# Two attention layers and two Fourier layers on one core: larger q/k pieces from step 234, and two more projection pieces before the end of the attention

## The chip, the cores and the metric

One core of a Trainium2 chip runs the whole program. The metric is the device time of one execution in microseconds (us), the median of several. Engines are named as in the profile: PE (matrix products), PEld (its weight loads), DVE (vector), ACT (activation), POOL, and SP, which here only issues DMA transfers.

## The reference

`x` has 2048 rows of 640 numbers. Four sublayers run one after the other, with `_A_ref` (attention) and `_B_ref` (Fourier mixing) used twice each:

```python
def _A_ref(x, wqkv, wo):                      # H = 32 heads of Dh = 20
    qkv = (x @ wqkv).reshape(B, S, 3, H, Dh).transpose(2, 0, 3, 1, 4)
    q, k, v = qkv[0], qkv[1], qkv[2]
    p = softmax(einsum("bhqd,bhkd->bhqk", q, k) * Dh ** -0.5)
    o = einsum("bhqk,bhkd->bhqd", p, v)
    return o.transpose(0, 2, 1, 3).reshape(B, S, D) @ wo

def _B_ref(x, dft_seq_re, dft_seq_im, dft_hid_re, dft_hid_im):
    a = einsum("bsd,ed->bse", x, dft_hid_re);  b = einsum("bsd,ed->bse", x, dft_hid_im)
    return einsum("ts,bse->bte", dft_seq_re, a) - einsum("ts,bse->bte", dft_seq_im, b)

x = A_x
x = x + _A_ref(_layernorm(x), A_wqkv, A_wo)
x = x + _B_ref(_layernorm(x), B_dft_seq_re, B_dft_seq_im, B_dft_hid_re, B_dft_hid_im)
x = x + _A_ref(_layernorm(x), A_wqkv, A_wo)
x = x + _B_ref(_layernorm(x), B_dft_seq_re, B_dft_seq_im, B_dft_hid_re, B_dft_hid_im)
```

## The kernel before, in words

The program has two equal layers, each an attention and a Fourier part. A layer runs in stages.

**Prologue.** The rows of x are normalised and transposed (`xt`), and q and k of the first 128 columns and half of v are computed.

**Attention** (`Attention.sweep`). There are 512 steps: 8 groups of 4 heads, 4 blocks of 512 query columns (`qb`), 16 blocks of 128 key rows (`kc`). A step has two *scores* (`s` in the tables: two matmuls into one of three PSUM tiles `psc`, and after them one exponential on ACT, `e<-psc`, into one of seven buffers `e`) and one *values* (`v`: four matmuls, which the chip runs as eight, that add `e` times `v` to `acc`). After `kc` 15, DVE empties `acc`, divides by the row sums and POOL stores the result `o` to DRAM. PE's order is the order in which these calls are written down, one after the other.

**Filling work** stands between the steps on PE. The remaining columns of q and k (`pqk<-xt,wqk`) are made in units of 15 matmuls of 512 columns, each unit ending in a small matmul for row norms (`pn<-sq,ind`). `pieces(…, n)` cuts a unit into pieces of n. Up to step 234 (`THIN` is 236) a written-out string sets the order: `f` is a piece, `n` a norm. This part is called *dense* below. From there on before.py puts one piece of 5 at steps `(n - 1) % 16` in 2, 7, 12 (`due`), 33 pieces, and leaves the rest to the rule in `sweep`.

**Projection pieces.** From step 448 the table `tail` gives strings for 5 to 8 steps each, with one `f` in each. Such a piece is `Project.begin(n, i)`: 9 matmuls of 320 columns (`py<-wo,o`) that multiply three fifths of the attention's output for row tile n, half i, by `wo`; DVE adds the result to the residual rows `xr`. There are ten pieces (row tiles 0 to 4, two halves each).

**Projection stage** (`Project.run`). For row tiles 0 to 15, two halves each, PE does what is left of the product: 6 matmuls a half for tiles that were begun, 15 for the others. DVE adds it to `xr` (`L1007`), then the pair of row tiles is stored to DRAM (`d_x<-xr`, in `moments`) and normalised and folded for the Fourier part. SP issues in program order, pair by pair: a load of `xr` three pairs ahead, which reuses the buffer of the pair before and so waits for that pair's store; after pairs 1 and 3 eight loads of `o` (`fetch`) for the row tiles 8 to 11 and 12 to 15; then the pair's own store.

**Fourier part.** PE multiplies by the two DFT matrices. Its products start when the folded rows are there.

Things that run beside all this: DVE's comparisons of the DFT matrices (`compare`), and `tasks`, one at every second step, which load and split `wo` and other weights after the last q/k piece.

Of the kernel before, what the change touches and what calls it, by code (L numbers as in the profile page):

```python
# [19 lines left out]
ND = D // 128  # L20
NT = S // 128
# [18 lines left out]
def mha_fnet_kernel(ctx, tc, x_in, wqk, wv, wo, seq, hid, nat_seq, nat_hid, out):  # L40
# [33 lines left out]
    def bank(tag, shape, name):  # L74
        return pools["pool"].tile(list(shape), F32, name=name, tag=tag)
# [60 lines left out]
    class Qkv:  # L136
# [119 lines left out]
        def begin(s, first, kq, vals, room, given):  # L256


            s.first, s.room, s.given, s.w = first, room, given, {}
            for k in range(2):  # L260
                if given:
                    s.raw[k * ND] = given.wraw[k]
                else:
                    s.load(k)
            s.wvraw = [vals(f"v{NT - 1 - dc}", [HD], F32, "wvraw") for dc in range(ND)]
            if given:
                s.load_values()
# [117 lines left out]
        def work(s):  # L385

            order = [ND + 1, 1, ND + 2, 2, ND + 3, 3, ND + 4, 4]
            w = {0: s.w1}

            def chunk(i):  # L390
                c = order[i]
                for tb in range(NB):
                    p = bank("fill", [128, 512], "pqk")
                    for more in pieces([s.product(p, w[i], tb, dc) for dc in range(ND)], 8 if (i, tb) < (5, 1) else 5):
                        if more:
                            yield True
                    sq = s.keep(p, c, tb, True, s.fill)

                    def after():
                        s.norms(bank("fill", [H, 512], "pn"), c, tb, sq)  # L400
                        s.made.add((c, tb))
                        if tb == NB - 1:
                            s.made.add(c)
                            if i + 1 < len(order):
                                w[i + 1] = s.weights(s.fill("w", [2, ND, 128], F32R, "wqk"), order[i + 1], True)
                            if i + 2 < len(order):
# [12 lines left out]
            s.made.add("v")  # L419
            for i in range(4, 8):  # L420
                yield from chunk(i)

            s.silent = True
            r = s.bounds()
            ok = const.tile([128, 1], F32, name="ok", bufs=2)
            V.tensor_scalar(ok[:H], r[:H, 2:3], (GUARD / SCALE) ** 2, None, op0=OP.is_le)

            def after():
                p = bank("fill", [1, 1], "pok")
                PE.matmul(p, ok[:H], one[:H], start=True, stop=True)  # L430
                V.tensor_scalar(s.flag, p, float(H), None, op0=OP.is_equal)
            yield after
# [25 lines left out]
    class Attention:  # L458
# [98 lines left out]
        def sweep(s, shift, begin, fill=lambda n: None, plan=None, block=None, compare=lambda n: None):  # L557
            done = calm = n = 0

            def opened(n):  # L560
                g, qb, kc = s.steps[n]
                begin(n, g, qb, kc)
                last = qb == NB - 1
                if kc == (7 if last else 10 if g in LATE else 4) and not (last and g == H // 4 - 1):
                    s.qload(*((g, qb + 1) if not last else (g + 1, 0)), shift)
                if last and g + 1 < H // 4:
                    for f, j in {1: [(0, 0)], 9: [(0, 1)], 11: [(1, 0)]}.get(kc, []):
                        s.kload(g + 1, f, j)
                if qb == 0 and kc == 0 and g:
                    s.kload(g, 1, 1)  # L570

            while n < len(s.steps):
                opened(n)
                order = plan and plan(n)
                if order:

                    while done < n - 1:
                        s.values(done)
                        done += 1
                    t = 2 * n  # L580
                    for c in order:
                        if c == "s":
                            m, j = divmod(t, 2)
                            if not j and m > n:
                                opened(m)
                            s.scores(m, j)
                            if j:
                                compare(m)
                            t += 1
                        elif c == "v":  # L590
                            s.values(done)
                            done += 1
                        else:
                            (block if c == "f" else fill)(t // 2)
                    n = t // 2
                    continue
                s.scores(n, 0)
                s.scores(n, 1)
                more, owed = fill(n) and n >= 2 and n + 1 < len(s.steps), n - 1 - done
                compare(n)  # L600
                n += 1
                if plan and n <= s.THIN:
                    count = owed + 1
                elif more and owed < 3:
                    calm = n + 1
                    continue
                else:
                    count = min(owed, 1)
                    if owed > 1 and (done + 1) % NT and n > calm:
                        calm = n + 1  # L610
                        count = 2
                for _ in range(count):
                    s.values(done)
                    done += 1
            for n in range(done, len(s.steps)):
                s.values(n)

        def run(s, done, project, check):
# [2 lines left out]
            s.work, s.blocks, s.after, s.rest, s.more, s.landed = True, 0, None, 0, False, 0  # L621


            tail, n = {}, 448
            for steps in (6, 7, 6, 8, 6, 6, 6, 6, 5, 8):
                tail[n] = {5: "sssfssvssvvsssvv", 6: "sssfssvssvssvvsssvv", 7: "sssfssvssvssvssvvsssvv",
                           8: "sssfssvssvsvssvssvssvssvv"}[steps]
                n += steps

            def due(n):  # L630
                return s.blocks < 58 or s.blocks >= 91 or (n - 1) % NT in (2, 7, 12)

            def block(n):
                if not s.work:
# [22 lines left out]
            def plan(n):  # L657
                if n in tail:
                    return tail[n]
                if s.blocks >= 58 or s.after:  # L660
                    return
                whole = 32 <= s.blocks < 48
                if n % 4 == 1 and n + (4 if whole else 8) < s.THIN and (whole or s.blocks % 2 == 0):
                    return "sssfsssvvssvv" if whole else "ssfsssvvsssvvsssfssvvsssnvv"
# [22 lines left out]
            def begin(n, g, qb, kc):  # L687
# [17 lines left out]
                for f in project.early.get(n, []):  # L705
                    f()

            s.sweep("b", begin, fill, plan, block, compare)
            assert not s.work and not later and not tasks and not project.parts, (len(later), len(tasks))

# [233 lines left out]
    class Project:  # L944
        def __init__(s, att, src, dst):
            s.att, s.src, s.dst, s.w, s.raw = att, src, dst, {}, {}
            s.sum = {}
            s.oh, s.x, s.xn, s.rs, s.f, s.g, s.nb, s.na = {}, {}, {}, {}, {}, {}, {}, {}

            s.begun, s.parts = set(), [lambda n=n, i=i: s.begin(n, i) for n in range(5) for i in range(2)]  # L950
            s.early = {474: [lambda: s.fetch(0, 0, 1)], 486: [lambda: s.fetch(1, 0, 0)], 503: [lambda: s.fetch(0, 1, 1)]}

        def weights(s, dc):

# [662 lines left out]
```

## Time and profile before

| what | value |
|---|---|
| median of 3 runs | 2460.21 us (2456.98 to 2460.39) |
| the profiled execution's own time | 2460.17 us |
| its span, first to last instruction | 2458.3 us |
| PE busy | 2428.5 us (99% of the span) |
| ACT busy | 2117.6 us (86%) |
| DVE busy | 995.3 us (40%) |
| exponentials `e<-psc` | 2048, one per half step |
| mean granted TensorE clock | 0.998 |

A row of a timeline or of a group names line, engine, operation, the tile written and the tiles read, and the shape; `x8` is the number of instructions merged in the row. Times are from the span's start. PE's busy time is modelled from pipelined matmuls that overlap, so it says little; the time from the start of one row to the start of the next says what PE needed. Line numbers are those of before.py.

### The profile page before, as it was taken

The numbers are of one execution on the slowest core, as the hardware profiler recorded it, in microseconds if no ns is written. First come the engines' busy times: TensorE is split into PE (matmuls) and PEld (weight loads), VectorE is DVE, ScalarE is ACT, GpSimd is POOL, SyncE is SP. The second block draws the span as 40 slices with busy tenths as digits, with TensorE's granted clock in tenths as the row PEclk, the third lists the DMA queues.
The fourth block names the chain that finished last, engine by engine and source line by source line (L and its number), as shares of the span: only waits on it lengthen the run. The fifth ranks groups of instructions, "written<-read, shape, count | busy, mean of one in ns | idle before, by whom it ended". The sixth has DMA issues, their size and how long they took to land. (4 is left out here: it accounts for less than half of the span.)

```text
span 2458.3 us, 43836 instructions
## 1 busy us (share of the span) xinstructions
PE 2428.5 (99%) x16350; PEld 1174.1 (48%) x16350; DVE 995.3 (40%) x2198; ACT 2117.6 (86%) x2428; POOL 527.7 (21%) x1032
## 2 busy tenths in 40 slices
PE   8999999999999999999999999999999999999997
PEld 7644444443333333349885444454433333333596
DVE  6244442234343333427763444323333232323275
ACT  6699998899999999995457989888999999999762
POOL 2012211112111212115321212211112212222143
PEclk9999999999999999999999999999999999999999
DMA  5324231223232225318552332312222322252274
GB/s 184 101 89 126 81 113 51 77 69 109 74 96 89 88 86 168 96 44 284 193 182 96 112 102 85 117 53 69 79 82 57 93 64 68 57 151 83 67 255 185
DMA packets 128228, 262.64 MB, mean 107 GB/s; under 512 B 29937, under 2 KB 54289, under 8 KB 128005
## 3 DMA queue, kind: packets, MB, share of 16 engines
q1 hardware_dynamic: 89412, 159.89, 20.4%
q0 software_dynamic: 38592, 99.85, 12.8%
q8 instruction: 132, 2.16, 0.4%
q14 instruction: 92, 0.75, 0.1%
HBM read 175.29 MB, written 84.31 MB: 106 GB/s over the span
## 5 line engine op out<-in xcount | busy, mean ns | idle before, releaser
L525 ACT ACTIVATE e<-psc 128x1024 f32<-128x1024 f32 x2048 | 1919.4, 1059 | 109.9 <-PE psc L522 98.9
L533 PE MATMUL acc<-e,v 128*32 128x512 f32 x8192 | 1034.2, 600 | 0.4 <-DVE of L540 0.4
L522 PE MATMUL psc<-stq,stk 62*128 62x512 f32 x4096 | 745.3, 445 | 2.3 <-ACT e L525 1.1
L522 PEld LDWEIGHTS psc<-stq,stk 62*128 62x128 f32 x4096 | 333.9, 184 | 704.2 <-ACT e L525 563.8
L533 PEld LDWEIGHTS acc<-e,v 128*32 128x32 f32 x8192 | 217.5, 108 | 396.3 <-issue 357.5
L103 PE MATMUL pqk<-xt,wqk 128*128 128x512 f32 x1200 | 319.4, 407 | 0.5 <-ACT xt L90 0.2
L554 POOL DMA_DIRECT2D o<-oh x256 | 131.2, 521 | 828.7 <-DVE oh L549 816.8
L88 DVE CAST hl<-pqk 128x512 fp32r<-128x512 f32 x64 | 44.3, 692 | 597.8 <-PE pqk L103 597.8
L103 PEld LDWEIGHTS pqk<-xt,wqk 128*128 128x128 f32 x1200 | 213.1, 188 | 84.1 <-issue 39.6
L103 PE MATMUL pv<-wv,xt 128*128 128x320 f32 x960 | 151.3, 313 | 0.0
L103 PEld LDWEIGHTS pv<-wv,xt 128*128 128x128 f32 x960 | 141.1, 188 | 15.5 <-issue 9.7
L554 POOL DMA_DIRECT2D o<-ot x256 | 128.2, 509 | 1.8 <-issue 0.9
L540 DVE STREAM_TRANSPOSE of<-acc 128x512 f32<-128x512 f32 x64 | 45.8, 715 | 199.2 <-PE acc L533 199.2
L211 POOL DMA_DIRECT2D scrq<-hl x40 | 28.3, 706 | 429.6 <-DVE hl L91 240.1
L211 POOL DMA_DIRECT2D scrk<-hl x40 | 27.7, 693 | 390.1 <-DVE hl L91 280.6
L96 PE MATMUL py<-wo,o 128*128 128x320 f32 x320 | 101.3, 316 | 2.3 <-DVE xr L1007 1.3
L217 DVE TENSOR_REDUCE top<-pn 32x1 f32<-32x512 f32 x80 | 53.6, 677 | 121.0 <-PE pn L216 120.6
L803 DVE TENSOR_REDUCE far<-cq 128x1 f32<-128x512 f32 (+5 forms) x169 | 98.5, 584 | 5.7
L98 PE MATMUL py<-wo,o 128*128 128x320 f32 x320 | 99.1, 310 | 1.0 <-DMA o<-o 1.0
L97 PE MATMUL py<-wo,o 128*128 128x320 f32 x320 | 98.7, 308 | 0.0
L807 DVE TENSOR_TENSOR cq<-cq 128x512 f32<-128x512 f32 (+4 forms) x166 | 96.3, 580 | 4.2 <-DMA cq<-in_nat_seq_dram 3.5
L247 DVE COPY v<-pv 128x320 f32<-128x320 f32 x32 | 15.7, 489 | 161.3 <-PE pv L103 161.3
(201 smaller groups left out, 1750.7 us busy)
## 6 DMA issues: line engine op xcount, KB each, us to landing
cq<-in_nat_seq_dram POOLq DMA_DIRECT2D x64, 512.0 KB, 5.4
scrq<-hl POOLq DMA_DIRECT2D x40, 512.0 KB, 3.2
scrk<-hl POOLq DMA_DIRECT2D x40, 512.0 KB, 3.2
stq<-scrq SPq DMA_DIRECT2D x256, 80.0 KB
stk<-scrk SPq DMA_DIRECT2D x128, 160.0 KB
o<-o SPq DMA_DIRECT2D x32, 384.0 KB
stq<-scrq SPq DMA_DIRECT2D x256, 40.0 KB
stk<-scrk SPq DMA_DIRECT2D x128, 80.0 KB
```

The lines of the kernel that those rows point to most:

```text
L96: PE.matmul(out_ap, ah, bh, start=start, stop=False)
L97: PE.matmul(out_ap, ah, bl, start=False, stop=False)
L98: PE.matmul(out_ap, al, bh, start=False, stop=stop)
L103: yield lambda i=i, j=j, k=k: PE.matmul(out_ap, a[i], b[j], start=dc == 0 and k == 0, stop=dc == ND - 1 and k == 2)
L211: G.dma_start(s.scr["qk"[k]][c * 128:(c + 1) * 128, :, tb * 512:(tb + 1) * 512], hl.bitcast(F32))
L217: V.tensor_reduce(s.top[:H, c // ND, c % ND, tb:tb + 1], p, op=OP.max, axis=AX.X)
L522: PE.matmul(p[:, i], s.k[g, kc // 8, j][r, kc % 8 * 128:(kc % 8 + 1) * 128], s.q[g, qb, j][r], start=True, stop=True)
L525: A.activation(e, p, AF.Exp, scale=SCALE)
L533: PE.matmul(s.acc[32 * j:32 * j + 32], s.a.v[kc][:, v0:v0 + 32], s.e[n, j // 2][:, j % 2], start=kc == 0, stop=kc == NT - 1, skip_group_ch ...
L554: G.dma_start(s.o[k, h * DH:(h + 1) * DH, qb * 512:(qb + 1) * 512], hl[k][32 * j:32 * j + DH])
L803: V.tensor_reduce(to, x, op=OP.max, axis=AX.X, apply_absolute_value=True)
L807: V.tensor_tensor(y, x, y, op=op)
```

## The change

Three edits.

1. The last 11 q/k units: `pieces` now cuts every unit into 8 and 7, so there are 22 pieces after the 58th where there were 33. `plan` gives a written-out string for every eight steps from step 234 to 410, with one piece in each, in place of `due` and the rule in `sweep`. (For strings that begin otherwise than `ss`, `sweep` no longer catches up on values first.)
2. `tail` starts at step 432 and has twelve strings, and the twelve projection pieces are those of row tiles 0, 1, 2, 3, 4 and 6. `Project.run` then does 6 matmuls a half for row tile 6.
3. The load of `o` that row tiles 4 and 6 share, `fetch(1, 0, 0)`, is issued at step 460 and not 486.

```diff
-                    for more in pieces([...], 8 if (i, tb) < (5, 1) else 5):
+                    for more in pieces([...], 8):
...
-                    while done < n - 1:
+                    while order[0:2] == "ss" and done < n - 1:
...
-            tail, n = {}, 448
-            for steps in (6, 7, 6, 8, 6, 6, 6, 6, 5, 8):
+            tail, n = {}, 432
+            for steps in (7, 6, 6, 6, 8, 6, 6, 6, 7, 7, 6, 6):
...
             def due(n):
-                return s.blocks < 58 or s.blocks >= 91 or (n - 1) % NT in (2, 7, 12)
+                return s.blocks >= 80
...
-                if s.blocks >= 58 or s.after:
+                if s.blocks >= 80 or s.after:
+                    return
+                if s.blocks >= 58:
+                    if n >= 234 and n % 8 == 2:
+                        if s.blocks == 58:
+                            return "sfsssvssvssvssvsvssvssvs"
+                        return "sfsssvvssvssvssvsvssvssvs" if s.blocks % 2 == 0 else "sfsssvvssvssvssnvsvssvssvs"
                     return
...
-            s.begun, s.parts = set(), [... for n in range(5) for i in range(2)]
-            s.early = {474: [lambda: s.fetch(0, 0, 1)], 486: [lambda: s.fetch(1, 0, 0)], 503: [...]}
+            s.begun, s.parts = set(), [... for n in (0, 1, 2, 3, 4, 6) for i in range(2)]
+            s.early = {474: [lambda: s.fetch(0, 0, 1)], 460: [lambda: s.fetch(1, 0, 0)], 503: [...]}
```

The order on PE in the part from step 234, first before (from step 264), then changed (from step 266). `psc` x4 is two scores, `acc` x4 one values, `pqk` a piece.

```order
L103 MATMUL pqk<-xt,wqk 128x512 x5
L522 MATMUL psc<-stq,stk 128x512 x4
L533 MATMUL acc<-e,v 32x512 x4
L522 MATMUL psc<-stq,stk 128x512 x4
L533 MATMUL acc<-e,v 32x512 x8
L522 MATMUL psc<-stq,stk 128x512 x4
L533 MATMUL acc<-e,v 32x512 x4
L522 MATMUL psc<-stq,stk 128x512 x4
L533 MATMUL acc<-e,v 32x512 x4
L522 MATMUL psc<-stq,stk 128x512 x4
L103 MATMUL pqk<-xt,wqk 128x512 x5
L522 MATMUL psc<-stq,stk 128x512 x4
```

```order
L103 MATMUL pqk<-xt,wqk 128x512 x8
L522 MATMUL psc<-stq,stk 128x512 x6
L533 MATMUL acc<-e,v 32x512 x8
L522 MATMUL psc<-stq,stk 128x512 x4
L533 MATMUL acc<-e,v 32x512 x4
L522 MATMUL psc<-stq,stk 128x512 x4
L533 MATMUL acc<-e,v 32x512 x4
L522 MATMUL psc<-stq,stk 128x512 x4
L533 MATMUL acc<-e,v 32x512 x4
L522 MATMUL psc<-stq,stk 128x512 x2
L533 MATMUL acc<-e,v 32x512 x4
L522 MATMUL psc<-stq,stk 128x512 x4
```

Pieces of 5 every five or six steps have become pieces of 8 and 7 every eight; a piece is now followed by three scores (x6) and a double values (x8), and each eight steps hold one score that stands alone (x2).

The order on SP around step 420, first before, then changed. `woraw` are loads of `wo`, `o` those of the attention's output, `shiftb` a store, and `stq` the next block's q.

```order
L503 DMA stq<-shiftb_69 2x512
L451 DMA shiftb_69<-sh 4x8x64
L958 DMA woraw<-in_wo_dram 128x640
L500 DMA stq<-scrq_67 40x1x512
L501 DMA stq<-scrq_67 20x512
```

```order
L503 DMA stq<-shiftb_69 2x512
L964 DMA woraw<-in_wo_dram 128x640 x2
L982 DMA o<-o_71 128x3x256 x2
L964 DMA woraw<-in_wo_dram 128x640
L982 DMA o<-o_71 128x3x256 x2
L451 DMA shiftb_69<-sh 4x8x64
L500 DMA stq<-scrq_67 40x1x512
```

The loads that the projection pieces need now stand ahead of a block's `shiftb` and `stq`, where one of them stood between and the others behind.

More of the change, by code (lines that the diff above doesn't have):

```diff
@@ L393, in chunk @@
                     p = bank("fill", [128, 512], "pqk")
-                    for more in pieces([s.product(p, w[i], tb, dc) for dc in range(ND)], 8 if (i, tb) < (5, 1) else 5):
+                    for more in pieces([s.product(p, w[i], tb, dc) for dc in range(ND)], 8):
                         if more:
@@ L948, in __init__ @@
             s.oh, s.x, s.xn, s.rs, s.f, s.g, s.nb, s.na = {}, {}, {}, {}, {}, {}, {}, {}
-            s.begun, s.parts = set(), [lambda n=n, i=i: s.begin(n, i) for n in range(5) for i in range(2)]
-            s.early = {474: [lambda: s.fetch(0, 0, 1)], 486: [lambda: s.fetch(1, 0, 0)], 503: [lambda: s.fetch(0, 1, 1)]}
+            s.begun, s.parts = set(), [lambda n=n, i=i: s.begin(n, i) for n in (0, 1, 2, 3, 4, 6) for i in range(2)]
+            s.early = {474: [lambda: s.fetch(0, 0, 1)], 460: [lambda: s.fetch(1, 0, 0)], 503: [lambda: s.fetch(0, 1, 1)]}
         def weights(s, dc):
```

## The prediction

> **What bounds the kernel now.** I read the stages first: the busy time of the instructions on the tile `e` (exponentials on ACT, values on PE) in four stretches of the first layer: steps 234 to 410, 410 to 432, 432 to 448, 448 to 512. The columns are the stretch, its length, then PE, PEld, DVE and ACT with their counts.
>
> ```profile
> 577.30:910.92 333.62, 181.92 (x1400) 31.83 (x1399) 0.00 (x0) 329.37 (x353) 1.00 0.28 87
> 910.92:951.20 40.28, 23.41 (x176) 3.67 (x176) 0.00 (x0) 40.10 (x44) 1.00 0.39 125
> 951.20:981.29 30.09, 17.91 (x136) 2.80 (x136) 0.00 (x0) 29.88 (x33) 1.00 0.61 183
> 981.29:1101.83 120.54, 64.80 (x516) 12.93 (x516) 0.00 (x0) 118.67 (x128) 1.00 0.25 70
> ```
>
> The second stretch holds nearly no filling work: 44 exponentials in 40.28 us, 0.9155 us each, 1.831 us a step. That is ACT's own pace. At it the first stretch (176 steps) would take 322.3 us, and it takes 333.6. The last two (80 steps) would take 146.5 and take 150.6. So 11.3 and 4.1 us per layer lie above ACT's pace, and only these, with the projection stage, can be touched. ACT's 99% there hides this: its rows overlap and swallow short waits.
>
> Who holds ACT up shows in the order of time on PE, in the first stretch:
>
> ```profile
> 721.77 0.73 PE L522 MATMUL psc<-stq,stk 62*128 62x512 f32 x4
> 722.43 1.45 PE L103 MATMUL pqk<-xt,wqk 128*128 128x512 f32 x5
> 723.81 0.73 PE L522 MATMUL psc<-stq,stk 62*128 62x512 f32 x4
> 724.47 1.07 PE L533 MATMUL acc<-e,v 128*32 128x512 f32 x8
> 725.47 0.73 PE L522 MATMUL psc<-stq,stk 62*128 62x512 f32 x4
> 726.13 1.93 PE L533 MATMUL acc<-e,v 128*32 128x512 f32 x16
> 727.99 0.73 PE L522 MATMUL psc<-stq,stk 62*128 62x512 f32 x4
> ```
>
> From start to start: two scores 0.66, one values 1.00, two values in a row 1.86, a piece of 5 1.38. The shapes that the new strings use stand in the dense part and, for a score alone, in the tail:
>
> ```profile
> 152.59 0.39 PE L216 MATMUL pn<-sq,ind 128*32 128x512 bf16 x1
> 152.59 2.10 PE L533 MATMUL acc<-e,v 128*32 128x512 f32 x16
> 154.62 0.73 PE L522 MATMUL psc<-stq,stk 62*128 62x512 f32 x4
> 155.28 2.11 PE L103 MATMUL pqk<-xt,wqk 128*128 128x512 f32 x8
> 157.32 0.97 PE L522 MATMUL psc<-stq,stk 62*128 62x512 f32 x6
> 158.22 1.92 PE L533 MATMUL acc<-e,v 128*32 128x512 f32 x16
> ```
>
> ```profile
> 1022.42 0.50 PE L522 MATMUL psc<-stq,stk 62*128 62x512 f32 x2
> 1022.86 1.06 PE L533 MATMUL acc<-e,v 128*32 128x512 f32 x8
> ```
>
> Three scores 0.90, one score 0.44, a piece of 8 2.04, a norm 0.17 (2.03 less 1.86). A further matmul in a piece is (2.04 - 1.38) / 3 = 0.22, so a piece of 7 is 1.82, and opening and closing a piece costs about 0.28.
>
> **Edit 1, steps 234 to 432.** PE's work in 16 steps before, by the strings: 16 pairs of scores 10.56, ten single values 10.00, three double ones 5.58, three pieces of 5 4.14, a norm 0.17: 30.45. The stretch gives 333.62 / 11 = 30.33, so PE is the bound there and works without gaps; ACT's 16 steps are 29.30. Changed: twelve pairs 7.92, two triples 1.80, two single scores 0.88, twelve single values 12.00, two double ones 3.72, pieces of 8 and 7 3.86, a norm 0.17: 30.35. One piece less saves 0.28, but the more broken order of scores and values gives back 0.18. The saving is 0.10 per 16 steps, 1.1 us over eleven periods.
>
> It is taken back at the far end. Before, the last piece of 5 and its norm came after step 410, where the second stretch goes at ACT's pace: they were free. The changed order has everything inside 234 to 410: 11 x 30.35 = 333.9 against 333.6, and 40.3 against 40.3 after it. That makes +0.3 us; from below it is -1.1 (if that piece still hides), from above +1.2 (if at the start, where the dense part hands over few exponentials in advance, the first piece of 8 also costs a wait as long as its own surplus over a piece of 5, 0.66, and a little more). I take +0.3, from the sum of rows.
>
> **Edit 2, steps 432 to 512.** Before, ten pieces cost the 4.1 us above ACT's pace, 0.41 each. Each is seen as a short wait between exponentials; an early one:
>
> ```profile
> 981.29 8.36 ACT L525 ACTIVATE e<-psc 128x1024 f32<-128x1024 f32 x9 [0.21 <-PE psc L522]
> 989.83 12.95 ACT L525 ACTIVATE e<-psc 128x1024 f32<-128x1024 f32 x14 [0.18 <-PE psc L522]
> ```
>
> Nine exponentials took 8.54 where 9 x 0.9155 is 8.24. Twelve pieces at 0.41 make +0.8 us. Bounds: 0, if PE's slack (1.831 less 1.66 per step) takes the two more; +2.6, the PE time of 18 matmuls, if none of it does. I take +0.8. The two more additions on DVE are of half a microsecond each and DVE is 40% busy; the moved loads (`woraw`, `o`) come two or more steps ahead of their users.
>
> **What is taken out of the projection stage.** Row tile 6 loses 18 matmuls. Their price, and what PE does six row tiles later (first layer, start of row tile 12; then the second layer):
>
> ```profile
> 1143.22 0.31 PE L97 MATMUL py<-wo,o 128*128 128x320 f32 x1
> 1143.37 0.31 PE L98 MATMUL py<-wo,o 128*128 128x320 f32 x1
> 1144.67 0.39 PE L96 MATMUL py<-wo,o 128*128 128x320 f32 x1 [0.99 <-DVE fold L1062]
> 1144.89 0.31 PE L97 MATMUL py<-wo,o 128*128 128x320 f32 x1
> 1145.71 0.41 PE L98 MATMUL py<-wo,o 128*128 128x320 f32 x1 [0.50 <-DMA o<-o]
> ```
>
> ```profile
> 2360.79 0.31 PE L97 MATMUL py<-wo,o 128*128 128x320 f32 x1
> 2361.61 0.41 PE L98 MATMUL py<-wo,o 128*128 128x320 f32 x1 [0.51 <-DMA o<-o]
> ```
>
> One matmul is 0.147 from start to start, 18 are 2.65 us per layer. PE otherwise runs this stage without gaps, so at first sight they are saved whole. But at row tile 12 PE stands still until `o` has landed: 1.15 and 0.67 us in the first layer, 0.67 in the second. The row names DVE for the first of these; the `o` load issued at 1139.57 is the later one. So I followed SP:
>
> ```profile
> 1121.62 0.82 SPq L1019 DMA_DIRECT2D d_x<-xr  x1
> ...
> 1129.83 0.38 SPq L997 DMA_DIRECT2D xr<-in_x_dram  x1
> 1130.31 0.42 SPq L1019 DMA_DIRECT2D d_x<-xr  x1
> 1139.11 0.37 SPq L997 DMA_DIRECT2D xr<-in_x_dram  x1
> 1139.57 4.91 SPq L976 DMA_DIRECT2D o<-o  x8
> ```
>
> and SP's own waits between 1102 and 1165, and what the DMA engines moved from 1116 to 1146 in 40 slices:
>
> ```profile
> SPq L997 <- DMA d_x<-xr: 25.9, 4, 8.2
> ...
> GB/s 10 58 283 263 294 378 376 374 348 355 347 344 350 348 365 421 424 431 393 426 415 395 285 341 369 416 234 31 24 24 0 0 79 229 317 376 384 370 362 350
> ```
>
> The chain is: store of pair 1 (1121.62) lands, load of `xr` (1129.83), store of pair 2 (1130.31) lands, load of `xr` (1139.11), eight loads of `o`, of which the first two let row tile 12 begin. SP waits 25.9 us for such stores, and they take 8 us because the engines move 350 to 430 GB/s through that time. PE stands in none of these links. So in the changed kernel PE comes to row tile 12 2.65 us earlier and waits 2.65 us longer; what follows starts when it did. The saving is 0. Bounds: 0 and -2.65 per layer. I take 0, since both layers show the wait.
>
> The Trainium skill, page "DMA: Bandwidth & Descriptors", section "Specifications", gives 358 GB/s per core from HBM as the limit; by that the chain would be later still. The row's 431 GB/s says otherwise, and either way the saving is 0.
>
> **Sum.** The profiled execution took 2460.17 us (span 2458.3), the median of the runs is 2460.21: the same. Per layer +0.3 + 0.8 + 0 = +1.1; two equal layers +2.2: **2462.4 us**. A measurement of this kernel can tell about 0.2% (4.9 us) from no change.
>
> **The rivals.**
>
> *The projection stage does save its matmuls.* For it: PE has no other gap there over 1 us, and a chain of DMAs can end a microsecond or two earlier or later (row tile 12 waits 1.2 us less in the second layer). Against: the chain. Time: 2 x (1.1 - 2.65) = -3.1, 2457.1. Chance 0.20. Half of it saved gives 2459.7.
>
> *The new order lets ACT run at its pace from step 234* (the pieces become free, as the one after 410 was). For it: fewer openings. Against: PE's own sum, 30.35 per 16 steps, is above ACT's 29.30. Time: up to 2 x 11.3 less, about 2442. Chance 0.07.
>
> *PE has to wait inside the new strings* (slower). Three `psc` tiles let PE be at most three scores ahead. A piece of 8 with the scores around it keeps ACT without a new score for 0.66 + 2.04 us and the time to the next score's end, about the 2.75 us of three exponentials; ACT runs dry, and afterwards PE, hurrying, finds the three tiles full and stands still. It decides if PE waits over 0.1 us per eight steps. At 0.3 us, 44 strings in both layers: +13, 2475. For it: three scores in a row come right after a piece. Against: PE is the longer of the two by a microsecond per 16 steps, so it seldom is ahead. Chance 0.12.
>
> *A piece's price is per matmul alone* (slower too): the 0.28 of opening and closing, drawn from two different parts of the kernel, is not there. Then the changed 16 steps cost 0.18 more and the moved piece still costs: 2 x (11 x 0.28) more than the sum, 2468.6. Chance 0.06. The Trainium skill, page "TensorE: Matmul & The Clock Gate", section "Back-to-back issue gap", has it so: N / 2.4 + 2.5 ns, 216 ns for 512 columns, without a term for the change of work. The rows above speak against it: 0.276 per matmul in a piece of 5, 0.255 in one of 8.
>
> *The change does not do what it says:* the built order shows 22 pieces, twelve projection pieces and row tile 6 with its rest. Nothing left, 0.
>
> Forecast: 0.55.
>
> **How the numbers follow.** Faster by over 0.2% (under 2455.3): ACT at its pace, and a part of the first rival where the runs scatter (three runs before lie 3.4 apart): 0.12. Slower by over 0.2% (over 2465.1): the two slower rivals, less the half of the second that stays below: 0.16. Within: 0.72. The range takes in the first rival and, above, the forecast with the upper bounds of its two terms at about half (+0.4 and +0.9 per layer, 2465): 2456 to 2466.
>
> **What would show it.** Right: steps 234 to 410 take 333 to 335 us, 410 to 432 40.3; steps 432 to 512 about 151.4; row tile 12's first matmul starts as long after the attention's end as before, with a wait 2.6 us longer; row tile 8 starts 2 us or more earlier. Wrong: row tile 12 starts over a microsecond earlier (first rival); exponentials at 1.831 us a step from 234 on (second); PE rows in the strings that start over 0.1 us late while ACT is busy (third); a piece of 8 with 0.28 less than here, beside a piece of 5 as before (fourth).

## The result, and the profile after

| kernel | median of 17 runs, us | lowest to highest |
|---|---|---|
| before | 2458.92 | 2456.98 to 2460.39 |
| changed | 2463.43 | 2460.23 to 2466.53 |

The ratio is 1.0018, 95% interval 1.0012 to 1.0025: slower by 4.5 us (3.0 to 6.1), inside what was called "within 0.2%". The profiled execution of the changed kernel took 2463.36 us (span 2461.6), 3.2 more than that of before. The line numbers of the changed kernel are six higher from the middle of `sweep` on: L976 is now L982, L997 is L1003, L1007 is L1013, L1062 is L1068.

The four stretches of the first layer's attention, instructions on `e` as before (stretch, length, then PE, PEld, DVE, ACT):

```profile
577.82:912.31 334.49, 184.29 (x1404) 30.99 (x1408) 0.00 (x0) 326.64 (x354) 1.00 0.29 88
912.31:953.00 40.69, 24.00 (x184) 3.58 (x176) 0.00 (x0) 40.48 (x46) 1.00 0.47 149
953.00:983.92 30.92, 15.11 (x120) 2.95 (x120) 0.00 (x0) 29.62 (x33) 1.00 0.51 151
983.92:1104.62 120.70, 65.49 (x528) 13.38 (x524) 0.00 (x0) 118.76 (x129) 1.00 0.23 66
```

Against 333.62, 40.28, 30.08 and 120.55 the first three lost 0.86, 0.41 and 0.84 us, the last 0.16. In the second layer the four differences are 0.87, 0.41, -0.09 and 0.30. ACT's rows show where the first stretch paid, at its very start (the number in brackets is the idle time before the row):

```profile
573.99 4.86 ACT L525 ACTIVATE e<-psc 128x1024 f32<-128x1024 f32 x5
580.15 14.78 ACT L525 ACTIVATE e<-psc 128x1024 f32<-128x1024 f32 x16 [1.30 <-PE psc L522]
595.08 15.00 ACT L525 ACTIVATE e<-psc 128x1024 f32<-128x1024 f32 x16 [0.15 <-PE psc L522]
610.46 14.79 ACT L525 ACTIVATE e<-psc 128x1024 f32<-128x1024 f32 x16 [0.39 <-PE psc L522]
```

One wait of 1.30 us, then 16 exponentials at a time with 0.15 and 0.39 between them. The pieces themselves cost on PE what was said, from start to start 2.04 for a piece of 8 and 1.83 for one of 7:

```profile
714.01 1.89 PE L103 MATMUL pqk<-xt,wqk 128*128 128x512 f32 x7
715.84 1.00 PE L522 MATMUL psc<-stq,stk 62*128 62x512 f32 x6
...
729.17 2.11 PE L103 MATMUL pqk<-xt,wqk 128*128 128x512 f32 x8
731.21 0.96 PE L522 MATMUL psc<-stq,stk 62*128 62x512 f32 x6
```

In the third stretch PE waits once for DVE, and DVE's rows in order of time tell why:

```profile
956.44 0.88 PE L522 MATMUL psc<-stq,stk 62*128 62x512 f32 x4
958.64 1.06 PE L533 MATMUL acc<-e,v 128*32 128x512 f32 x8 [1.32 <-DVE of L540]
```

```profile
954.89 0.49 DVE L997 TENSOR_TENSOR xr<-py,xr 128x320 f32<-128x320 f32 x1 [12.82 <-PE py L98]
955.30 0.68 DVE L813 TENSOR_TENSOR cq<-cq 128x512 f32<-128x512 f32 x1
956.01 0.69 DVE L809 TENSOR_REDUCE far<-cq 128x1 f32<-128x512 f32 x1
956.62 0.48 DVE L88 CAST wo<-woraw 128x640 fp32r<-128x640 f32 x1
957.13 0.82 DVE L91 TENSOR_TENSOR wo<-woraw,wo 128x640 fp32r<-128x640 f32 x1
957.88 0.71 DVE L540 STREAM_TRANSPOSE of<-acc 128x512 f32<-128x512 f32 x1
```

The values of step 432 open a new `acc`; PE may write it when DVE has emptied the old one (L540). In DVE's order the addition of the first projection piece stands ahead of that, and it waits 12.8 us for the piece; behind it come a compare and a split of `wo`. All of them are short, and PE waits for the last.

In the projection stage row tile 6 takes 1.76 us and not 4.40 (from its first matmul to that of the next tile), 2.64 saved. The next tile takes 5.35, since at row tile 8 PE waits for DVE:

```profile
1127.01 0.41 PE L96 MATMUL py<-wo,o 128*128 128x320 f32 x1 [0.79 <-DVE xr L1013]
```

SP's chain of stores, loads and `o` fetches, first the first layer, then the second:

```profile
1105.81 2.97 SPq L982 DMA_DIRECT2D o<-o  x6
...
1132.93 0.41 SPq L1025 DMA_DIRECT2D d_x<-xr  x1
1140.35 0.37 SPq L1003 DMA_DIRECT2D xr<-in_x_dram  x1
1140.77 5.10 SPq L982 DMA_DIRECT2D o<-o  x8
...
2323.02 2.96 SPq L982 DMA_DIRECT2D o<-o  x6
...
2357.52 5.04 SPq L982 DMA_DIRECT2D o<-o  x8
```

And the two ends of it in the kernel before:

```profile
1103.03 2.96 SPq L976 DMA_DIRECT2D o<-o  x6
...
2320.17 2.96 SPq L976 DMA_DIRECT2D o<-o  x6
...
2355.36 5.00 SPq L976 DMA_DIRECT2D o<-o  x8
```

From the first `o` row to the last eight it was 36.54 us (to 1139.57, quoted in the prediction) and is 34.96; in the second layer 35.19 and 34.50. The chain came 1.58 and 0.69 us earlier by itself: row tile 6 stands in none of its links. Counted from the attention's end, row tile 12 begins 1.34 and 0.75 us earlier, row tile 13 1.35 and 0.67. That is the most that the 2.65 us per layer can have become; whether it is row tile 6's doing is taken up below, where the prediction is gone through.

The sum of the profiles: +0.52 ahead of step 234 (it begins at 577.82, not 577.30), attention +2.27 and +1.50, projection -1.35 and -0.67, the first Fourier part -0.09, the second +1.09 (see the end): +3.3, the difference of the two spans.

### The profile page after: what moved, and what is told of

It is laid out like the page before. It is cut to its first block, busy times and chain, and to the rows that moved or that the text cites. A ratio compares the mean times of both kernels' runs of the same rounds, so it can differ in the third digit from the quotient of the medians.

```text
span 2461.6 us, 43843 instructions
## 1 busy us (share of the span) xinstructions
PE 2426.8 (99%) x16350; PEld 1175.4 (48%) x16350; DVE 995.1 (40%) x2202; ACT 2113.0 (86%) x2428; POOL 532.7 (22%) x1032
## 5 line engine op out<-in xcount | busy, mean ns | idle before, releaser
L103 PE MATMUL pqk<-xt,wqk 128*128 128x512 f32 x1200 | 312.9, 404 | 0.0
L540 DVE STREAM_TRANSPOSE of<-acc 128x512 f32<-128x512 f32 x64 | 45.8, 716 | 482.9 <-PE acc L533 482.9
L103 PE MATMUL pv<-wv,xt 128*128 128x320 f32 x960 | 151.4, 313 | 0.0
```

Of the source, the lines that this page charges most:

```text
L103: yield lambda i=i, j=j, k=k: PE.matmul(out_ap, a[i], b[j], start=dc == 0 and k == 0, stop=dc == ND - 1 and k == 2)
```

## The experiments

My theory: edit 1 pays at its entry and gains a little where its last piece was; edit 2 costs 0.4 us a piece and, in the first layer, one wait for DVE's order; row tile 6 wins what SP's chain lets it win. The rivals: the strings themselves are slower; the pieces cost nothing and only waits do; DVE, not SP, bounds the projection stage. Between kernels whose order is the same in a stretch of the attention, its length repeats within 0.33 us, mostly within 0.1, so stretches are read for what the whole time can't tell. "From step 234" below means up to the start of the last exponential plus its own length; before has 524.54 in both layers, the changed kernel 526.81 and 526.04.

**Edit 1 alone (`e1_qk`).** The tail's table, ten pieces and step 486 as in before.

> The kernel before with edit 1 alone (q/k in pieces of 8 and 7 in written strings from step 234 to 410); the ten projection pieces, their table and the load at step 486 are as before. Theory (edit 1 pays once at its entry and once for the piece that no longer hides): steps 234 to 410 take 334.5 us (before 333.62), 410 to 432 40.7 (40.28), 432 to 512 150.6 as before, row tile 6 4.40 and row tile 12 as late as before; in all 2 x 1.28 = +2.6 us, so 2461.5. Rival (the strings of edits 1 and 2 disturb each other): 234 to 410 at 333.6 and the loss of the changed kernel comes from the twelve pieces; the time is that of before, 2459.

2460.96 us against 2459.91, ratio 1.0004 (0.9995 to 1.0013). From step 234 it takes 525.05 and 525.10: +0.51 and +0.56, not +1.28. The second stretch tells why:

```profile
577.29:911.76 334.47, 184.28 (x1404) 30.98 (x1408) 0.00 (x0) 326.61 (x353) 1.00 0.29 88
911.76:951.61 39.85, 23.15 (x176) 3.30 (x168) 0.00 (x0) 39.85 (x45) 1.00 0.51 166
```

Without before's last piece of 5, steps 410 to 432 take 39.85 and not 40.28: that piece, with its norm, had cost 0.43. And the changed kernel's 40.69 there holds the start of its tail, not a cost of edit 1 (`e2_no6` below, whose tail also starts at step 432, takes 40.71 there).

**Ten pieces in the changed kernel (`e2_no6`).**

```diff
-            for steps in (7, 6, 6, 6, 8, 6, 6, 6, 7, 7, 6, 6):
+            for steps in (8,) * 10:
...
-            s.begun, s.parts = ... for n in (0, 1, 2, 3, 4, 6) ...
+            s.begun, s.parts = ... for n in range(5) ...
```

> The changed kernel with ten projection pieces (row tiles 0 to 4) in ten strings of 8 steps from step 432; row tile 6 keeps all its matmuls. Theory: steps 234 to 432 as in the changed kernel (375.2 us); 432 to 512 has two pieces less, 2 x 0.41 us below the changed kernel's 151.6 (first layer) and 150.6 (second), so near before's 150.6 in the first and 149.8 to 150.5 in the second; row tile 6 takes 4.40 again and row tile 12 begins as late after the attention's end as in the kernel before, 1.34 and 0.68 us later than in the changed one. In all about +0.4 us against the changed kernel. Rival (the pieces cost nothing, the emptied accumulator and the loads do): 432 to 448 stays at 30.9 in the first layer, and the tail is not faster than in the changed kernel; +2.0 against it.

2463.02 us, ratio to before 1.0011 (1.0002 to 1.0020). From step 234 526.31 and 525.32, so two pieces less are worth 0.50 and 0.72 us. Steps 432 to 448 took 31.29 in the first layer: the wait for DVE is there with ten pieces as with twelve, as the rival had it for that place. In the projection stage row tile 14 begins 0.55 us earlier than in before in the first layer and 0.07 later in the second, so what the changed kernel won there is mostly gone. Row tile 12 did not behave as the theory said: in the first layer it began 1.16 us earlier than in before, though all of row tile 6's matmuls were in place; the chain was shorter there too (35.32 us). Gain and loss are under a microsecond per layer each, and the whole can't tell them apart.

**The task at step 434 held back (`e5_hold`).**

```diff
-                if tasks and n % 2 == 0 and n >= 16 and n % 64 < 54:
+                if tasks and n % 2 == 0 and n >= 16 and n % 64 < 54 and n != 434:
```

> The changed kernel, in which no task (a load or a split of a weight) is put at step 434; the split of wo that stood there comes two steps later, behind DVE's emptying of acc. Theory (PE waits 1.3 us for DVE to empty acc, because the addition of the first projection piece, two compares and that split stand before it on DVE): steps 432 to 448 take 30.0 us in the first layer, 0.9 less, and nothing changes in the second, which waits only 0.4 us; -0.9 us in all, 2462.5. Rival (the wait is set by the first projection piece itself, which is late behind scores and values): 30.9 again, 2463.4.

Steps 432 to 448 take 29.88 us in both layers, 1.03 and 0.12 less:

```profile
954.37 0.49 DVE L997 TENSOR_TENSOR xr<-py,xr 128x320 f32<-128x320 f32 x1 [12.60 <-PE py L98]
...
956.10 0.70 DVE L540 STREAM_TRANSPOSE of<-acc 128x512 f32<-128x512 f32 x1
```

With the split gone from its front, the transpose of `acc` starts 1.73 us after the addition and not 2.99. From step 234 525.76 and 525.91 are left. But the whole did not gain: 2464.41 us (ratio to before 1.0016, 1.0008 to 1.0025), not to be told from the changed kernel's 1.0018. In the profile, of an execution of 2461.94 us, row tile 13 begins 48.09 and 46.99 us after the attention, 1.16 and 0.63 later than in the changed kernel, since SP's chain took 36.17 and 35.35 us here and not 34.96 and 34.50. In this execution what was won ahead of the chain was lost in it.

**The eight `o` loads first (`e3_first_before`, `e4_first_after`).**

```diff
-                if p:
+                if p and p != 3:
                     s.load(p + 3)
...
                             s.fetch(p // 2 + 2, m, part)
+                    if p == 3:
+                        s.load(p + 3)
```

On the kernel before:

> The kernel before, with one swap in the projection stage: at pair 3 the eight loads of o for row tiles 12 to 15 are issued ahead of the load of xr that waits for a store, not behind it. Theory (PE stands at row tile 12 only because of that order on SP): row tiles 11 and 12 take 4.40 us each, 2.2 us less in the first layer and 0.95 less in the second; about -3 us, 2456. Rival (the loads of xr come later behind the eight loads, and DVE and PE wait for xr at a later row tile, or the Fourier part starts when it did): row tiles 11 and 12 go faster and later ones slower by as much; 2459.

2457.05 us, ratio 0.9989 (0.9980 to 0.9998): faster. SP's rows:

```profile
1103.55 2.96 SPq L976 DMA_DIRECT2D o<-o  x6
...
1129.96 0.41 SPq L1019 DMA_DIRECT2D d_x<-xr  x1
1130.48 9.12 SPq L976 DMA_DIRECT2D o<-o  x8
1139.77 0.59 SPq L997 DMA_DIRECT2D xr<-in_x_dram  x1
```

The loads are issued 26.93 us after the first `o` row, not 36.54, and row tiles 11 to 14 take 4.40 us each in both layers. No row tile is longer for the load of `xr` that now stands behind. On the changed kernel:

> The changed kernel with the same swap (the eight loads of o ahead of the waiting load of xr at pair 3). Theory (the 2.65 us of row tile 6 are eaten by the same wait for o): row tiles 11 and 12 take 4.40 to 4.5 us each, about 2.0 less in the first layer and 1.6 less in the second; 3.6 us below the changed kernel, 2460. Rival (DVE's pace from row tile 7 on is the bound, as its 0.95 us wait at row tile 8 shows): the wait for o goes but PE then waits for DVE as long; under 1 us gained.

2459.20 us, ratio to before 0.9996 (0.9987 to 1.0005), where the changed kernel has 1.0018. Row tiles 11 and 12 take 4.40. Row tiles 7 to 10 stay slow (5.36, 4.50, 5.58, 4.51 in the first layer). With the swap in both, row tile 6 begun early wins 0.29 us in the first layer and 1.43 in the second (row tile 13 at 45.78 and 44.65 after the attention, against 46.06 and 46.08), of 2.65. So the rival's "under 1 us gained" is wrong for the swap, but it is right about the rest: PE no longer waits for `o`, only for DVE (2.5 and 1.5 us in all), and behind SP's chain stands DVE's order.

**That order (`e9_six_early`).** The two additions of row tile 6 ahead of the fold of pair 0 and the sums of pair 2 on DVE; PE's order is unchanged.

```diff
-                for n in (2 * p, 2 * p + 1):
+                for n in {2: (4, 5, 6), 3: (7,)}.get(p, (2 * p, 2 * p + 1)):
                     s.product(n)
```

> The changed kernel with one move on DVE in the projection stage: the two additions of row tile 6 stand ahead of the fold of pair 0 and of the sums g of pair 2, not behind them; PE's order is the same. Theory (PE waits 0.95 us at row tile 8 because the additions of the short row tile 6 stand in DVE's order behind a fold that waits 3.3 us for POOL): row tile 7 takes 4.40 us and not 5.35, and row tile 12 still waits for its loads, now as much longer; no gain in the whole, 2463.4. Rival (DVE is short of time there, not blocked): row tile 7 still takes 5.3, or 8 and 9 take the difference. In both the whole is the changed kernel's within 0.3 us.

DVE in the changed kernel ahead of the additions of row tile 6 (the last row), which shows what they stood behind:

```profile
1123.86 0.56 DVE L1068 SCALAR_TENSOR_TENSOR fold<-g,ars,na 128x321 f32<-128x321 f32 x1 [3.27 <-POOL ars L1034]
...
1126.46 0.48 DVE L1013 SCALAR_TENSOR_TENSOR xr<-py,xr 128x320 f32<-128x320 f32 x1
```

Row tiles 7 and 8 take 4.40 again, in both layers: DVE was blocked there, not short of time, as the theory said. But the rival's second sign came in part: row tile 9 takes 6.78 in the first layer, since PE waits 2.17 us for an addition, and on DVE that addition stands behind two waits for ACT (2.92 and 1.74 us). That is again an order, not a want of time. Row tile 10 takes 6.04 for another reason, the clock:

```profile
1136.63 0.47 PE L96 MATMUL py<-wo,o 128*128 128x320 f32 x1 [2.17 <-DVE xr L1013]
1136.90 0.47 PE L97 MATMUL py<-wo,o 128*128 128x320 f32 x1
```

Its matmuls start 0.27 us apart and not 0.147; the granted clock was 0.50 from 1136.85 to 1140.26. The whole is 2463.40 us (ratio to before 1.0010, 1.0001 to 1.0018), the changed kernel's time; the profiled execution, 2466.56, was the slowest of the eleven. In its second layer row tile 12 took 9.04: its loads of `o` landed late, and the clock was at 0.50 for 6.83 us of it.

**Edit 1 with its strings from step 242 (`e6_qk242`).**

```diff
-                    if n >= 234 and n % 8 == 2:
+                    if n >= 242 and n % 8 == 2:
```

> The kernel before with edit 1 alone, its written strings beginning at step 242 and not 234 (22 strings, the last piece near step 411). Theory (the first piece of 8 costs a wait of about 1 us because the dense part hands over too few exponentials in advance; eight steps without a piece give that advance): steps 234 to 410 take 333.5 us or less, 1.0 below the kernel with strings from 234; 410 to 432 takes 40.3, 0.43 more, since the last piece now falls there; -0.6 per layer, 2459.8. Rival (PE is short of time throughout and the wait only moves to the first string at 242): 334.5 or more and 40.3, no gain, 2461.5.

2522.91 us, ratio 1.0252 (1.0238 to 1.0265). I had expected at worst no gain. ACT's rows:

```profile
593.96 14.77 ACT L525 ACTIVATE e<-psc 128x1024 f32<-128x1024 f32 x16 [0.91 <-PE psc L522]
610.38 14.93 ACT L525 ACTIVATE e<-psc 128x1024 f32<-128x1024 f32 x16 [1.64 <-PE acc L533]
627.15 14.87 ACT L525 ACTIVATE e<-psc 128x1024 f32<-128x1024 f32 x16 [1.84 <-PE acc L533]
```

Steps 234 to 410 take 363.0 us (29.4 more than in before; from step 234 to the end of the attention it is 31.4 more), and every string of eight steps waits 1.64 or 1.84 us, no longer for scores but for values. The first written string holds seven values for eight steps, the others eight. Counted in PE's rows, scores are ahead of values by 1.5 steps at the first piece of edit 1 alone and by 2.5 at all later ones; at step 242 they were ahead by 2.5 already, and from the second piece on by 3.5. Two exponentials a step, 3.5 steps: seven buffers `e`, all of them full.

**The same with eight values in the first string (`e10_owed`).**

```diff
-                        if s.blocks == 58:
-                            return "sfsssvssvssvssvsvssvssvs"
```

> As the kernel with edit 1 alone and strings from step 242, but its first string has eight values like the others, not seven, so that PE owes 2.5 steps of values at each piece and not 3.5. Theory (29 us per layer were lost because 3.5 owed steps of two exponentials fill all seven buffers e, and ACT then waits for PE's values once per string): the waits go; steps 234 to 410 take 333.4 to 334.0 us, without the 1.1 us that the entry at 234 costs, 410 to 432 takes 40.3; 2459 to 2460, the time of the kernel before. Rival 1 (the strings need step 234 for another reason): 360 us or more again. Rival 2 (the entry's wait is owed to the first piece of 8 wherever it stands): 334.5, 2461.

2459.27 us, ratio 1.0000 (0.9991 to 1.0009).

```profile
577.75:911.23 333.48, 184.14 (x1400) 30.87 (x1400) 0.00 (x0) 326.25 (x354) 1.00 0.28 87
911.23:951.72 40.49, 23.40 (x176) 3.66 (x176) 0.00 (x0) 40.20 (x46) 1.00 0.39 120
```

Scores are 2.5 steps ahead at every piece, the waits are gone, and from step 234 it takes 524.55 and 524.53: before's time to 0.01 us. ACT still stands idle for 0.92 us at the first piece of 8, with 2.5 steps of lead, where the changed kernel had 1.30 with 1.5. So rival 2 is right that this piece brings a wait wherever it stands; but the eight steps ahead of it, which now hold no piece, go without a wait of ACT and make up for it (steps 234 to 250 take 30.34 us, against 30.11 in before and 31.19 in the changed kernel). In the sum it no longer shows: 333.48 and 40.49 against 333.62 and 40.28.

**Twelve pieces from step 448 on the kernel before (`e7_late12`).**

```diff
-            for steps in (6, 7, 6, 8, 6, 6, 6, 6, 5, 8):
+            for steps in (6, 5, 5, 6, 5, 5, 6, 5, 5, 6, 5, 5):
```

> The kernel before with edits 2 and 3 in part: twelve projection pieces (row tile 6 among them) in twelve strings of 5 and 6 steps from step 448; q and k are cut and placed as before, the load stays at step 486. Theory (a piece costs 0.4 to 0.5 us above ACT's pace wherever it stands): steps 234 to 448 as before (403.98 us), 448 to 512 takes 0.8 to 1.0 more than 120.54; in the projection stage the same -1.3 and -0.7 as in the changed kernel; 2459 to 2460. Rival (pieces every five steps leave PE no slack, so each costs its whole time): 448 to 512 takes 2.6 more, 2462.5.

2466.95 us, ratio 1.0024 (1.0015 to 1.0033). Steps 448 to 512 take 2.5 and 3.0 us more: the rival. ACT waits 0.34 to 0.43 us at all but the first two strings, not 0.2; two of them:

```profile
1009.15 11.13 ACT L525 ACTIVATE e<-psc 128x1024 f32<-128x1024 f32 x12 [0.34 <-PE psc L522]
1020.70 9.27 ACT L525 ACTIVATE e<-psc 128x1024 f32<-128x1024 f32 x10 [0.42 <-PE psc L522]
```

In this table, of strings of 5 and 6, a wait is twice as long as in the tables of mostly 6 to 8, and behind a string of 6 it is no shorter (0.42 in the second row, behind 12 exponentials). The other half of the theory failed too: the projection stage did not give -1.3 and -0.7. Row tile 13 began 0.61 and 0.47 us later than in before, with row tile 6 begun early; in the first layer the clock was at 0.50 for 3.41 us of it, in the second it was not.

**Three versions put together.** The changed kernel with the held task and the swap (`e11_hold_first`):

> The changed kernel with both repairs: no task at step 434, and the eight loads of o ahead of the waiting load of xr at pair 3. Theory: the 1.0 us of steps 432 to 448 stay won, because PE at row tile 12 no longer waits for SP's chain that ate them when the task alone was held; row tile 12 takes 4.4; 1.1 below the kernel with the swap alone, 2458. Rival (something else in the projection stage has a fixed time, such as DVE's queue at row tiles 7 to 10): the gain is eaten there again, 2459.2.

2457.72 us, ratio 0.9992 (0.9983 to 1.0001). 525.75 and 525.92 from step 234, row tile 13 at 44.84 and 45.11: in this profile the first layer keeps its microsecond. The medians can't tell it from the kernel with the swap alone (ratios 0.9992 and 0.9996). The strings of `e10_owed` with the swap and ten pieces (`e12_owed_first`):

> The kernel before with the q/k strings of the kernel that begins them at 242 and owes 2.5 steps, and with the eight loads of o ahead of the waiting load of xr at pair 3; ten projection pieces from step 448 as before. Theory (the strings are worth nothing and cost nothing once the entry is repaired, the swap is worth its 2.2 and 0.95 us): attention 524.5 us from step 234 as before, row tiles 11 and 12 4.4 us; 2456 to 2457, like the swap alone (2457.05). Rival: the strings' own saving of 0.1 us per 16 steps appears, 2455.

2456.86 us against 2458.73, ratio 0.9990 (0.9981 to 0.9999): faster than both kernels, and by no more than the swap alone. Its attention takes 524.53 in both layers. The same with twelve pieces in strings of 6 from step 440 (`e13_all`):

> The same with twelve projection pieces, row tile 6 among them, in twelve strings of 6 steps from step 440, the load for tiles 4 and 6 at step 460, and the weights' tasks allowed up to step 448. Theory: the two pieces cost 0.8 us per layer in the attention and win 2.65 less what DVE's queue holds back at row tiles 7 to 9 (1.2 to 2.4): 0.4 to 1.2 us per layer gained at most where the swap frees row tile 12; 2455 to 2457. Rival (strings of 6 leave PE too little slack, as strings of 5 and 6 from 448 did, where the attention lost 2.4 and 3.0 us): 2458 to 2460, slower than the same kernel with ten pieces.

2463.81 us, ratio 1.0022 (1.0013 to 1.0032): the rival's time and more, but not its reason. From step 234 528.70 and 528.51 us, 4.2 and 4.0 over the same kernel with ten pieces; row tile 13 came only 0.9 us earlier per layer. Most strings wait 0.2 us on ACT, four wait longer, each behind a wait of PE for `acc` (ACT's rows, then PE's, then one of DVE):

```profile
987.67 11.11 ACT L525 ACTIVATE e<-psc 128x1024 f32<-128x1024 f32 x12 [1.23 <-PE psc L522]
...
1022.14 11.11 ACT L525 ACTIVATE e<-psc 128x1024 f32<-128x1024 f32 x12 [0.58 <-PE psc L522]
```

```profile
986.07 1.06 PE L533 MATMUL acc<-e,v 128*32 128x512 f32 x8 [0.84 <-DVE of L540]
1018.03 1.07 PE L533 MATMUL acc<-e,v 128*32 128x512 f32 x8 [0.44 <-DVE of L540]
...
1045.10 1.06 PE L533 MATMUL acc<-e,v 128*32 128x512 f32 x8
1047.01 1.07 PE L533 MATMUL acc<-e,v 128*32 128x512 f32 x8 [0.84 <-DVE of L540]
```

```profile
1046.23 0.72 DVE L540 STREAM_TRANSPOSE of<-acc 128x512 f32<-128x512 f32 x1 [4.70 <-PE acc L533]
```

Three of PE's four waits, 0.84 us each, are alike (the third is shown; the fourth is at 1079.18). The strings of 6 put a double value right across the end of a block: PE does the last values of the old block and at once the first of the new one (no scores between 1045.10 and 1047.01), and DVE can begin to empty `acc` only when the old block's last values are there. DVE was idle before that, 4.70 us at the third. So this is not the changed kernel's case at step 433; only the second wait, 0.44 us, is like it, with the addition, a compare and a split of a weight ahead of the emptying. ACT's four waits (1.23, 0.58, 0.91, 1.23) are 3.2 us above four of 0.18: most of the 4. From step 432 on, PE has no such wait over 0.15 us in before, and in the changed kernel only the one at step 433 (1.32 us, in the second layer 0.38). That other strings would win the 3 us is read from these rows; no run tried it.

## Why the prediction was right, point by point

**The number.** 2462.4 forecast, 2463.43 measured, in the band that was given 0.72. The change itself was forecast too small: +2.2, measured +4.5 (3.0 to 6.1). That the time came so near is in part luck: in the profile the attention lost 3.8 us where 2.2 were said, and the projection stage gave back 2.0 that were not said.

**Edit 1, +0.3 per layer taken: +0.5 measured by itself.** The prices of the pieces and of three scores hold. The step that failed is "they were free", of the last piece before: `e1_qk` puts 0.43 us on it. The row that was called ACT's own pace, 40.28 us for 44 exponentials, held that piece; without it the pace is 39.85 / 44 = 0.906. So the far end gave back 0.43 where 0.3 loss was said. The entry cost what the upper bound named: steps 234 to 250 take 31.19 us, 1.08 more than before. The reason named there (too few exponentials handed over) is shown only in part: with one step more of lead the first piece of 8 still brings a wait of 0.92 us, and it is the eight steps without a piece that make up for it (`e10_owed`). What I did not follow is that the first string's missing value fits step 234 and no other, as `e6_qk242` and `e10_owed` show.

**Edit 2, +0.8 taken: +0.71 and +0.81 (`e5_hold` less `e1_qk`), plus 1.05 us once.** The price per piece came out right, for this table and in part by luck: 0.41 was drawn against the pace of 0.9155, and against 0.906 the same sum gives 0.57 a piece and +1.1. What failed is the sentence that trusts in a DVE that is 40% busy. It was not the two more additions: the wait is there with ten pieces too (`e2_no6`). The first piece's addition, now at step 433, and a split of `wo` behind it came ahead of the emptying of `acc`; with the split behind the emptying the wait went (`e5_hold`). DVE did not run out of time; its instructions wait for those ahead of them, as these rows show. Busy share says nothing on that.

**The projection stage, 0 taken: -1.35 and -0.67.** The mechanism was right: PE waits at row tile 12 for `o`, behind SP's chain, and the swap that breaks the chain gains 2.2 and 0.95 us in row tiles 11 and 12. The step that failed is "what follows starts when it did": the chain's length was taken for fixed, and it was 34.5 to 36.5 us over the profiles without the swap: 35.49 in the first layer of `e10_owed`, 1.05 shorter than in before, with nothing changed in the projection stage (row tile 13 came 1.02 us earlier there). Three of the signs failed with it: row tile 12 began 1.34 and 0.75 us earlier, in the first layer by more than the microsecond that was to speak for the first rival; row tiles 11 and 12 together lost 2.07 and 1.66 us, where before lost 2.20 and 0.95, and not 2.6 more; and row tile 8 started 1.69 us earlier and not 2, by DVE's order at that tile.

Nor is it shown that the 1.35 and 0.67 us come from row tile 6. Without the swap, row tile 14 of the first layer began 51.6 to 52.8 us after the attention in the five profiles with row tile 6 whole, and 51.3 to 53.3 in the four with it begun early (in two of these the clock was at 0.50 for 3.41 us of the stage). The changed kernel's 51.3 is the lowest of them all, so part of its gain may be chance; with one profile a kernel, the worth of row tile 6 and the chain's own spread can't be told apart. Only with the swap does it stand clear: row tile 13 comes at 46.06 to 46.08 us in all four layers of `e3_first_before` and `e12_owed_first`, and 0.3 to 1.4 us earlier in the six of `e4_first_after`, `e11_hold_first` and `e13_all`.

**The rivals.** The first (the matmuls are saved) came to 2.0 of its 5.3 us in the number; its reason is not shown. The second (ACT at its pace) did not come: 0.15 and 0.39 us stay between groups of 16. (Its time, "about 2442", does not follow from 2 x 11.3 us less, which gives under 2440; nothing else rests on it.) The third (PE waits inside the strings) did not happen in the changed kernel, but it lay one owed step away: `e6_qk242` lost 31 us per layer. I had its wall wrong; it is the seven buffers `e`, not the three `psc`. The fourth (no price for opening a piece) would give 11 x 0.18 = 2 us more per layer; `e10_owed` takes before's time, so the price is there.

**What would show it.** Steps 234 to 410: 333 to 335 said, 334.5. 410 to 432: 40.3 said, 40.7, with the start of the tail in it. 432 to 512: 151.4 said, 151.6 and 150.9.

## What to carry to other kernels

When work is taken from an engine, look for the next thing that has an order, not for the next busy engine: here a load queued behind one that waits for a store, and an addition queued behind a fold that waits for POOL, ate most of 2.65 us, and swapping two groups of DMA issues won 2.7 us on the kernel before, where the three edits lost 4.5. A chain of transfers can be a microsecond longer or shorter from one profile to the next, as SP's was here, so a gain of that size in one profile shows little. A hand-written order holds numbers that nothing checks: how many steps of values PE owes (shift the strings by eight steps and it can cost 31 us per layer), and where a block ends inside a string. Before calling a piece of work free because it lies in a fast stretch, take it out once; the fast stretch may be fast in spite of it.

## What was not expected of the hardware

In the last Fourier part of the changed kernel the granted clock falls to one half for 3.41 us, after two short waits of PE:

```profile
2404.17 0.50 PE L96 MATMUL pacc<-chl,xn 128*128 128x512 f32 x1 [1.26 <-DVE u L91]
2409.48 1.25 PE L1259 MATMUL pturn<-one,c3raw 1*128 1x1 f32 x12 [0.86 <-DVE c3raw L1251]
```

```profile
2411.19:2414.60 3.41, 3.41 (x10) 2.23 (x10) 0.78 (x5) 0.83 (x5) 0.00 (x0) 0.50 0.16 61
```

The column before the last two is the granted clock: 0.50 over 3.41 us, which is 1.7 us of full clock. From the last matmul of the projection to the end it took 80.33 us there and 79.23 in before. The one other profile with the first of these waits (1.95 us long there) and a half clock behind it, `e4_first_after`, took 80.43; the five with that wait and the clock at 1.00, `e5_hold` and `e9_six_early` among them, which hold the whole change, took 78.86 to 79.23. So the 1.1 us go with the clock and are not the change's. In five more profiles (`e2_no6`, `e7_late12`, `e10_owed`, `e11_hold_first`, `e12_owed_first`) the clock was at 0.50 for 3.41 us in this place behind the second wait alone; in `e6_qk242` and `e13_all`, with the same wait, it was not. The Trainium skill, page "TensorE: Matmul & The Clock Gate", section "What's actually happening", describes a free-running window of about 3.4 us over which it is judged how busy PE was, and a half clock after an idle one; the length of the stretch agrees, and that it comes in some profiles and not in others fits. The Trainium skill's rule in the same page's section "Why this matters for your kernels", no idle gaps over about 3 us, would not have warned here: the gaps were 1.26 and 0.86 us.
